# First pair's blocks inverted as halves of 16 tokens with a three-step solve, and a new order of the queues: a DeltaNet layer with a cosine-gated feed-forward

## The chip, the cores and the metric

The kernel runs on one core of one Trainium2 chip. The core has TensorE (PE, matmuls), VectorE (DVE), ScalarE (ACT), GpSimd (POOL) and SyncE (SP, which here only issues DMAs). The metric is the device time in microseconds of one launch.

## The reference

First a DeltaNet attention: 4 batches, 8 heads, 768 tokens, head size 48. Each head keeps a 48x48 state that is corrected token by token. Then each token's 384 features go through a feed-forward with 2048 hidden features and the gate h * cos(h).

```python
k_n = k / (norm(k) + 1e-06)
for t in range(S):
    y[:, :, t] = einsum('bhd,bhde->bhe', q[:, :, t], state)
    v_old      = einsum('bhde,bhd->bhe', state, k_n[:, :, t])
    state      = state + beta[:, :, t] * einsum('bhd,bhe->bhde', k_n[:, :, t], v[:, :, t] - v_old)
x = y as (3072 tokens, 384)
h = x @ w_in                 # 384 x 2048
out = (h * cos(h)) @ w_out   # 2048 x 384
```

The feed-forward weights arrive as float64 and are narrowed on the chip.

## The kernel before

**Tiling.** The 768 tokens of every head are cut into 24 units of 32 tokens (C = 32, unit n). Within a unit the token recursion is a unit triangular system: the Gram matrix of the unit's keys, scaled by beta, gives one 32x32 block for each of the 32 batch-head combinations. Two units make a pair m (12 pairs), whose 64 blocks are inverted together: half of the partitions holds the even rows of a block's inverse and the other half the odd ones.

**The recursion of one unit.** `turn` transposes keys and queries on TensorE (`turn_out` copies them on ScalarE). `gram` multiplies keys with keys and queries (L596). `gram_keys` scales the result on VectorE to `g` (L607), and `gram_put` sends `g` to memory (L634). For a pair, `gram_get` brings the blocks back as `gb`, with one block per partition (L643). `invert` runs over the 31 columns of the blocks with two instructions each, a product `part` and a subtraction from `z` (L672, L679). Pair 0 does this on VectorE with `z` in PSUM (`VECTOR = {0: "h"}`), the other pairs on GpSimd. `put` sends the inverse to memory (L688) and `get` brings it back as `zt` (L697). `solve` multiplies `zt` with the right-hand side (L745), `solve_out` scales it to `u` (L755), `update` and `update_out` change the state (L768, L776), `within` adds the unit's own part to its output (L785), and `features` transposes the output for the feed-forward (L804). `through_state` (L714) and `right_side` (L729) of the next unit need the new state.

**The feed-forward.** The pairs 0 and 1 run their hidden layer plainly: `hidden` (L825) makes 512 hidden features of 128 tokens with 12 matmuls, eight such groups to a pair, named by f = 0, 2, ..., 14. Pair 0 also has plain output groups (`output`, L970, four matmuls of 384 columns each). The later work uses a Strassen-like scheme (`layer`, L944, and `product`, L1027). Gating goes `turns` (ScalarE, L865), `rest` (VectorE, L872), `cos` (ScalarE, L881), `gate` (VectorE, L884).

**Weights.** There are 28 loads, 12 of w_in (512 KB) and 16 of w_out (384 KB). A load is `narrow_load` on SP (L465), `narrow_split` on ScalarE (L473, L475), `narrow_shift` on VectorE (L479, L484) and `narrow_add` on GpSimd (L488). A hidden group needs the adds of the w_in tiles up to its own part (f = 0 needs tiles 0 to 2, f = 6 needs all twelve); an output group needs those of w_out.

**What sets the order.** All tasks are handed to a list scheduler (`Order`) in the kernel's own source, each with an engine, a cost, a due time, the tasks it depends on, and the buffers it makes and frees. `Order.run` plays the engines with these costs and a model of DMA, and emits each task when its model starts it. The instructions of each engine, SP's included, then stay in exactly this order on the chip. `NUDGE` shifts due times by kind of task; the numbers were found by a search outside the kernel. The tag "g" is a pool of eight 4 KB buffers shared by weights, squares and gates.

Of the kernel before, what the change touches and what calls it, by code (L numbers as in the profile page):

```python
# [17 lines left out]
C = 32  # L18
# [7 lines left out]
def _consts():  # L26

    p = np.arange(128)
    share = p // 64
    row = SPLIT * np.arange(C // SPLIT)[None, :] + share[:, None]
    return np.concatenate(
        [
            np.eye(128),
            p[:, None] % C < np.arange(C)[None, :],
            p[:, None] // C % 2 == np.arange(2)[None, :],  # L40
            (row[:, :, None] == np.arange(C)).reshape(128, -1),
        ],
        axis=1,
    ).astype(np.float32)


class Order:
# [9 lines left out]
    WINDOW = 818.445  # L57
    LAG = {"PE": 0.2, "DVE": 0.15, "ACT": 0.15, "POOL": 0.2, "SP": 2.0, "IN": 0.0}
    IN_FLIGHT, ISSUE = 8, 0.49

    STEADY, LATE = 130.0, {"SP": 3.0, "POOL": 2.0}
    SLOW, WARM = 1.7, 4.0
    STICK = 1.823
    CHANGE = 0.15

    EARLY, NUDGE = 6, {('state', True): -3.4, ('features', False): -48.4, ('left', True): 37.6, ('solve', True): -19.7, ('turn', False): 12.2, ('within', True): -6.1, ('features_out', True): 39.0, ('rest', False): -12.6, ('weigh', False): -49.2, ('gram_put', True): 12.6, ('collect', False): -26.2, ('within', False): -32.5, ('features', True): -14.4, ('gate', True): -24.7, ('layer_out', False): -12.4, ('update', True): -10.5, ('sum', False): 24.3, ('layer', False): -1.8, ('add', True): -24.4, ('cos', True): 15.7, ('update', False): -6.1, ('solve', False): -34.1, ('norms', True): -9.2, ('state', False): -9.6, ('sum', True): 20.5, ('right', True): 24.7, ('hidden', True): 17.1, ('blocks', False): 2.6, ('gram', False): -8.1, ('inv_out', False): -15.0, ('v', False): 17.4, ('out', True): -13.0, ('eye', True): -0.5, ('features_out', False): -17.0, ('within_out', False): -0.6, ('gram_get', False): 12.2, ('gram_get', True): -21.0, ('turns', True): 8.1, ('scale', True): 5.8, ('k', True): -20.2, ('shift', True): -4.8, ('shift', False): 2.4, ('collect', True): 0.5, ('out', False): 0.3, ('scale', False): -1.8, ('out_out', True): 0.9, ('weigh', True): 5.0, ('store', True): -5.1, ('split', False): 9.0, ('within_out', True): -1.7, ('turns', False): -10.9, ('store_right', True): 3.6, ('turn_out', True): 1.5, ('k', False): 0.9, ('store_right', False): -5.1, ('inv', False): 5.4, ('square', False): 7.4, ('square', True): 4.1, ('norms', False): -1.3, ('store', False): 3.3, ('hidden', False): -4.1, ('cos', False): 3.4, ('x_sum', False): -0.6, ('beta_home', False): -1.9, ('store_left', True): -3.3, ('get', False): -6.1, ('get', True): 4.0, ('in_sums', False): 2.9, ('gram_queries', True): 1.6, ('turn_out', False): 5.0, ('update_out', False): -0.3, ('store_left', False): 0.1, ('inv', True): 1.1, ('v', True): -0.9, ('eye', False): -2.2, ('x_sum', True): 0.7, ('split', True): -3.1, ('beta_home', True): -4.7, ('weights', True): -0.3, ('gate', False): -3.7, ('put', False): -1.3, ('inv_out', True): -1.1, ('gram_keys', True): 0.6, ('solve_out', False): -1.5, ('add', False): 1.0, ('in_sums', True): 0.3}
# [5 lines left out]
    SMALL = ("gram", "state", "solve", "update", "within")  # L72
# [4 lines left out]
        "turn": 16, "gram": 128, "state": 256, "solve": 128, "update": 64, "within": 128,  # L77
# [8 lines left out]
    def add(  # L86
        self, key, engine, cost, emit, deps=(), makes=(), uses=(), moves=0.0, due=1e9
    ):

        assert key not in self.tasks, key  # L90
        self.tasks[key] = [engine, cost, due, emit, set(deps), makes, uses, moves]
        for t in uses:
            self.users[t] = self.users.get(t, 0) + 1
        for tag, t in makes:
            self.tiles[t] = tag
# [7 lines left out]

    def stall(self, key, now, commit):
# [5 lines left out]
        for i in range(self.written + 1, self.written + n + 1):  # L110
            t = now + cost * (i - self.written) / n + stall
            if (i + self.PHASE + self.AHEAD) % self.BLOCK == 0:
                there[(i + self.PHASE + self.AHEAD) // self.BLOCK + 1] = t + self.FETCH
# [10 lines left out]
    def run(self, wrote):  # L124
# [16 lines left out]
        for key, task in self.tasks.items():  # L141
# [3 lines left out]
            task[2] += self.NUDGE.get((key[0], n < self.EARLY), 0.0)  # L145
# [6 lines left out]
        flights, dma_free, hot = [5.5] * 4 + [8.5] * 4, 8.0, 1e9  # L152
        running, small = {}, False
        events = [(t, 0, None, False) for t in sorted(set(free.values()) | {0.0})]
# [3 lines left out]
        while events:  # L158
# [28 lines left out]
            for engine, heap in ready.items():  # L187
                if free[engine] > now:
                    continue
                able = [x for x in heap if x[0] <= limit and fits(x[2])]  # L190
# [39 lines left out]
                if moves:  # L230
                    end, parts = now, max(1, round(cost / self.ISSUE))
                    for _ in range(parts):
                        end = max(end, flights[-self.IN_FLIGHT]) + self.ISSUE
                        dma_free = max(dma_free, end + 0.5) + moves / parts
                        flights.append(dma_free + 1.4)
                    done = flights[-1]
# [12 lines left out]
def kernel(  # L249
# [85 lines left out]


# [14 lines left out]
    def qp(n):  # L351
        return qps[n // 2 % len(qps)][:, n % 2]

# [39 lines left out]
    near = 130 + C  # L393
# [4 lines left out]
    eye = consts[:, 130 + C :].rearrange("p (r i) -> p r i", i=C)  # L398
# [5 lines left out]
    nc.gpsimd.dma_start(out=consts[:, near:], in_=consts_dr.ap()[:, near:])  # L404

# [55 lines left out]
    def narrow_load(t):  # L461
# [3 lines left out]
        nc.sync.dma_start(out=words[t], in_=src)  # L465
# [147 lines left out]

    def gram_queries(n):
# [8 lines left out]
    def gram_put(n):  # L623
        m = n // 2
        if m not in gbs:
            gbs[m] = dram.tile([2, H, B, C, C], FP, name="g_dr")
# [6 lines left out]
        for rows, heads, bs in parts:  # L633
            nc.sync.dma_start(  # L634
# [3 lines left out]
    def gram_get(m):  # L638

        g_dr = gbs[m]  # L640
        gbs[m] = work.tile([128, C, C], FP, name="gb", bufs=GBS)
        for a in range(SPLIT):
            nc.sync.dma_start(  # L643
# [4 lines left out]
    def invert_eye(m, tag):  # L648
        if tag is None:
            zs[m] = work.tile([128, ROWS, C], FP, name="z", bufs=ZS)  # L650
        else:
            zs[m] = bank(tag, [128, ROWS, C], "p_i")
        nc.scalar.copy(zs[m], eye)

    def invert(m, tag, columns):
# [6 lines left out]
        for j in columns:  # L662
            rows = j // SPLIT + 1
            shape = [128, rows, C - 1 - j]
# [16 lines left out]
    def invert_out(m):  # L681
        z = work.tile([128, ROWS, C], FP, name="z", bufs=ZS)
        nc.scalar.copy(z, zs[m])
        zs[m] = z

    def put(m):
        z_drs[m] = dram.tile([ROWS, SPLIT, 2, H, B, C], FP, name="z_dr")
        nc.sync.dma_start(  # L688
# [3 lines left out]
    def get(n):  # L692

        zts[n] = work.tile([128, H, C], FP, name="zt")
        z_dr = z_drs[n // 2].rearrange("r s u h b i -> u b (r s) h i")[n % 2]
        for b in range(B):
            nc.sync.dma_start(out=zts[n][quarter(b)], in_=z_dr[b])  # L697
# [25 lines left out]
    def right_side(n):  # L723
# [10 lines left out]
        )  # L734

# [368 lines left out]
    W_IN, W_OUT, LOADS = 24.824, 4.888, 290.255  # L1104
    ONES, PLAIN = range(2), range(1)
    outs_done, collected, layered = [None], [None], [None]
    START = 41.528
    FIRST, STEP = 2.12, 3.854
    BASE = [START + (8 * FIRST + (p - 1) * 8 * STEP if p else 0) for p in range(NU // 2 + 2)]

    def inverse(m):
        add(("gram_get", m), "SP", 1.2, lambda: gram_get(m),
            [("gram_put", 2 * m), ("gram_put", 2 * m + 1)], makes=[("gb", ("gb", m))],
            uses=[("g_dr", m)], moves=1.6)
# [4 lines left out]
            makes=[(held or "z", z)])  # L1119
        deps = [("eye", m), ("gram_get", m)]  # L1120
        ends = [0, 4, 8, 12, 16, 20, 24, C - 1]
        for i, (x, y) in enumerate(zip(ends, ends[1:])):
            each = (0.2, 0.001) if held else (0.323, 0.00178)
            cost = sum(
                2 * (each[0] + each[1] * (j // SPLIT + 1) * (C - 1 - j)) for j in range(x, y)
# [3 lines left out]
                uses=[("gb", m)] if y == C - 1 else [])  # L1129
# [8 lines left out]
    def unit(n):  # L1138
        m, second = n // 2, n % 2
        for x, prev in (("k", 2 * len(kps)), ("q", 2 * len(qps)), ("v", 4)):  # L1140
# [7 lines left out]
            if x != "v" and n >= prev:  # L1148
# [5 lines left out]
                (x, n), "SP", 3.9 if x == "k" and n >= PLAIN_TURNS else 1.95,  # L1154
                lambda x=x: load(n, x), deps,
# [5 lines left out]
        if n < 4 or not second:  # L1161
# [8 lines left out]
            add(("scale", m, a), "DVE", 1.2, lambda: scale(m, part),  # L1170
                [("norms", m, a), ("beta",) if n < PLAIN_TURNS else ("beta_home",)])
        scaled = ("scale", m, a if n < 4 else 0)
        if second:
            add(("weigh", m), "DVE", 1.0 if n < PLAIN_TURNS else 1.35, lambda: weigh(m),
# [3 lines left out]
        if n < PLAIN_TURNS:  # L1178
            add(("turn", n), "PE", 0.9, lambda: turn(n, tag),
# [6 lines left out]
        else:  # L1186
            for a in range(2):
                deps = [("blocks", n - 1, a)] if n > PLAIN_TURNS else [("turn_out", n - 1)]
                deps.append(("turn_out", n - len(blocks)))
                add(("blocks", n, a), "SP", 1.9, lambda a=a: load_blocks(n, a), deps,  # L1190
# [4 lines left out]
        add(("gram", n), "PE", 0.75, lambda: gram(n, tag),  # L1195
# [5 lines left out]
            uses=[("p_g", n), ("scales", m)])  # L1201
        add(("gram_queries", n), "DVE", 0.46, lambda: gram_queries(n), [("gram_keys", n)],
            uses=[("p_g", n)])
        add(("gram_put", n), "SP", 0.45 if n < PLAIN_TURNS else 1.35, lambda: gram_put(n), [("gram_keys", n)],
            makes=[] if second else [("g_dr", ("g_dr", m))], uses=[("g_gram", n)],
            moves=0.85)
        if second:
            inverse(m)
        add(("get", n), "SP", 1.9, lambda: get(n), [("put", m)], makes=[("zt", ("zt", n))],
            uses=[("z_dr", m)], moves=0.9)  # L1210

        add(("state", n), "PE", 1.3 if n else 0.0, lambda: through_state(n),
# [5 lines left out]
        few = 0.75 if n < PLAIN_TURNS else 0.52  # L1218
        add(("solve", n), "PE", few, lambda: solve(n), [("right", n), ("get", n)],
            makes=[("two", ("p_u", n))], uses=[("zt", n), ("rhs", n) if n else ("vp", m)])  # L1220
# [12 lines left out]
        add(("features", n), "PE", 0.35, lambda: features(n), [("within_out", n)],  # L1233
# [5 lines left out]
    def gating(p, f, deps, uses, makes, due):  # L1239
        key = (p, f)  # L1240
        add(("turns", *key), "ACT", 0.65, lambda: hidden_turns(p, f), deps,
            makes=[("turns", ("turns", *key))])
        add(("rest", *key), "DVE", 0.73, lambda: hidden_rest(p, f), [("turns", *key)])
        add(("cos", *key), "ACT", 1.45, lambda: hidden_cos(p, f), [("rest", *key)])
# [17 lines left out]
    def gated(p):  # L1262
# [3 lines left out]
        for s in range(2):  # L1266
# [3 lines left out]
            for i in range(8):  # L1270
# [8 lines left out]
                add(key, "PE", 0.875 * count, lambda s=s, i=i: layer(p, s, i), deps,  # L1279
# [119 lines left out]
    def weights(t):  # L1399
        c = 1.0 if t < 12 else 0.8  # L1400
# [86 lines left out]
```

## Time and profile before

| what | value |
|---|---|
| time, median of 3 runs | 673.01 us (670.65 to 675.20) |
| the profiled execution | 673.73 us, its span 672.0 us |
| granted TensorE clock, mean | 0.992 |
| TensorE busy | 611.2 us (91%) |
| VectorE, ScalarE, GpSimd busy | 476.5, 246.6, 347.1 us |
| DMA | 52.55 MB, 215515 packets |

The page divides the span into 40 slices of 16.8 us and gives for each the busy share in tenths. A timeline row has start and length in us, the engine, the line, the operation, the output and inputs with their shapes, the count, and in brackets the idle time of the engine before it with what ended that. TensorE's float32 matmuls count twice in the trace, as each makes two passes. "PE", "DVE", "ACT" and "POOL" are the engines named above, and SPq is SP's queue of DMA issues.

### The profile page before, as it was taken

The page shows a single profiled execution, that of the slowest core. Times are in us where ns is not written, and L with a number is a line of the kernel's source. Part 1 is how long each engine was busy: PE and PEld are TensorE (multiplying, and loading weights), DVE is VectorE, ACT ScalarE, POOL GpSimd, SP SyncE. Part 2 cuts the span into 40 slices and gives each one's busy share as a digit, 9 for nine tenths or more (in the row PEclk, how much of TensorE's full clock was granted, in tenths as well). Part 3 has the DMA queues.
Part 4 walks back from the last instruction along what each step waited for, and adds up shares of the span by engine and source line. Part 5 has one row for each costly group of instructions (what it writes and reads, how often), then busy time and mean ns, then how long its engine had stood idle before and what let it go on. Part 6 is the DMA issues. An engine that isn't in the chain of part 4 may idle for free.

```text
span 672.0 us, 27226 instructions
## 1 busy us (share of the span) xinstructions
PE 611.2 (91%) x11864; PEld 572.8 (85%) x11864; DVE 476.5 (71%) x913; ACT 246.6 (37%) x414; POOL 347.1 (52%) x734
## 2 busy tenths in 40 slices
PE   4303798999999999999999999999999999999997
PEld 3202687986899999999999999999999999999996
DVE  5799498977676785886876876776766666656661
ACT  4432356551133342542432433433333334333420
POOL 4369797986848428587285383482382670000000
PEclk9999798999999999999999999999999999999999
DMA  8897655465453463434524524515213202000000
GB/s 179 198 199 158 155 130 161 103 115 90 68 96 65 63 101 59 90 56 68 109 36 60 113 34 65 107 26 92 56 21 57 56 7 54 1 4 24 1 24 24
DMA packets 215515, 52.55 MB, mean 78 GB/s; under 512 B 206948, under 2 KB 210164, under 8 KB 215396
## 3 DMA queue, kind: packets, MB, share of 16 engines
q1 hardware_dynamic: 212964, 49.98, 38.6%
q8 instruction: 93, 1.52, 1.0%
q10 hardware_dynamic: 2176, 0.39, 0.4%
q0 software_dynamic: 256, 0.44, 0.3%
q14 instruction: 26, 0.21, 0.1%
HBM read 39.76 MB, written 11.01 MB: 76 GB/s over the span
## 4 chain that ended last, share of the span: by engine, by line
PE 82%; POOL 7%; DMA 4%; DVE 2%; issue 2%; ACT 1%; SPq 1%; POOLq 0%; ACTq 0%
PE p_h L944 30%; PE p_out L1027 29%; PE p_kq L714 4%; PE p_h L825 4%; PE p_out L970 3%; PE p_u L745 2%; PE p_s L768 2%; PE p_kq L785 2%; PE p_g L596 2%; POOL part L672 2%; POOL z L679 2%; DMA gb<-g_dr 2%; POOL knrm L517 2%; PE p_o L1027 2%; POOL w_in L488 1%
## 5 line engine op out<-in xcount | busy, mean ns | idle before, releaser
L672 POOL TENSOR_TENSOR part<-z,gb 128x126 f32<-128x126 f32 (+22 forms) x341 | 136.0, 399 | 106.4 <-DMA gb<-g_dr 64.2
L679 POOL TENSOR_TENSOR z<-z,part 128x126 f32<-128x126 f32 (+22 forms) x341 | 137.3, 403 | 26.7
L944 PE MATMUL p_h<-x_ffn,w_in 128*128 128x128 f32 x1120 | 143.4, 277 | 0.0
L944 PEld LDWEIGHTS p_h<-x_ffn,w_in 128*128 128x128 f32 x1120 | 135.4, 192 | 1.2
L1027 PE MATMUL p_out<-w_out,g_ffn 128*128 128x192 f32 x672 | 123.8, 329 | 1.0 <-issue 1.0
L865 ACT ACTIVATE turns<-p_h,quarter_turn 128x512 int32<-128x512 f32 x96 | 65.8, 686 | 130.4 <-DVE p_h L963 96.2
L1027 PEld LDWEIGHTS p_out<-w_out,g_ffn 128*128 128x128 f32 x672 | 107.6, 190 | 1.7 <-issue 0.5
L1027 PE MATMUL p_out<-w_sum,g_ffn 128*128 128x192 f32 x496 | 91.6, 329 | 0.0
L881 ACT ACTIVATE turns<-turns,halfpi 128x512 f32<-128x512 f32 x96 | 69.1, 721 | 46.6 <-DVE turns L872 45.9
L872 DVE SCALAR_TENSOR_TENSOR turns<-p_h,turns 128x512 f32<-128x512 f32 x96 | 65.6, 684 | 23.4 <-ACT turns L865 23.3
L1027 PEld LDWEIGHTS p_out<-w_sum,g_ffn 128*128 128x128 f32 x496 | 79.3, 190 | 0.9
L1043 DVE TENSOR_TENSOR g_ffn<-g_ffn 128x512 f32<-128x512 f32 x88 | 63.2, 719 | 13.6 <-PE p_out L1027 13.3
L517 POOL TENSOR_TENSOR knrm<-ksum,halves 128x16 f32<-128x16 f32 (+1 forms) x14 | 37.2, 2657 | 66.7 <-DVE ksum L505 66.7
L884 DVE TENSOR_TENSOR g_ffn<-turns,p_h 128x512 f32<-128x512 f32 x96 | 65.0, 679 | 7.5 <-ACT turns L881 6.6
L963 DVE TENSOR_TENSOR p_h<-g_ffn,p_h 128x512 f32<-128x512 f32 x60 | 41.7, 695 | 40.0 <-PE p_h L944 37.9
L960 ACT COPY g_ffn<-p_h 128x512 f32<-128x512 f32 x60 | 35.1, 584 | 77.7 <-PE p_h L944 77.6
L825 PE MATMUL p_h<-x_ffn,w_in 128*128 128x128 f32 x384 | 47.6, 282 | 0.7 <-POOL w_in L488 0.6
L825 PEld LDWEIGHTS p_h<-x_ffn,w_in 128*128 128x128 f32 x384 | 45.2, 196 | 2.1 <-POOL w_in L488 1.1
L1077 DVE SCALAR_TENSOR_TENSOR o<-p_out,o 128x192 f32<-128x192 f32 x74 | 25.2, 353 | 28.9 <-PE p_out L1027 27.6
L944 PE MATMUL p_h<-x_sum,in_sum 128*128 128x128 f32 x320 | 43.7, 280 | 0.0
L944 PEld LDWEIGHTS p_h<-x_sum,in_sum 128*128 128x128 f32 x320 | 39.5, 192 | 1.1
L755 DVE TENSOR_TENSOR u<-p_u,bz 128x384 f32<-128x384 f32 x48 | 24.5, 552 | 14.9 <-PE p_u L745 14.6
(95 smaller groups left out, 759.0 us busy)
## 6 DMA issues: line engine op xcount, KB each, us to landing
pairs<-in_moe_w_in_dram SPq DMA_DIRECT2D x12, 512.0 KB
gb<-g_dr SPq DMA_DIRECT2D x24, 256.0 KB
pairs<-in_moe_w_out_dram SPq DMA_DIRECT2D x16, 384.0 KB
vp<-in_v_dram SPq DMA_DIRECT2D x96, 48.0 KB
out_dram<-o SPq DMA_DIRECT2D x23, 192.0 KB
z_dr<-z SPq DMA_DIRECT2D x12, 256.0 KB
zt<-z_dr SPq DMA_DIRECT2D x96, 32.0 KB
kp<-in_k_dram SPq DMA_DIRECT2D x128, 24.0 KB
```

What stands on the lines that cost most here:

```text
L517: nc.gpsimd.tensor_tensor(out=scales[m][2][:, part], in0=sums[m, part.start][:, 0:n], in1=halves[:, 0:n], op=ALU.pow,)
L672: eng.tensor_tensor(out=part, in0=z[:, 0:rows, j, None].to_broadcast(shape), in1=a[:, j, None, j + 1 :].to_broadcast(shape), op=ALU.mult,)
L679: eng.tensor_tensor(out=behind, in0=behind, in1=part, op=ALU.subtract)
L825: nc.tensor.matmul(p_h[:, i], w_in[:, t, (4 * k + i) * 128 : (4 * k + i + 1) * 128], xts[p][:, t, unit * 128 : (unit + 1) * 128], start=(t ...
L865: nc.scalar.activation(turns[p, f], hidden_of(p, f), AF.Identity, bias=quarter_turn, scale=TURN)
L872: nc.vector.scalar_tensor_tensor(out=r, in0=hidden_of(p, f), scalar=TURN, in1=t, op0=ALU.mult, op1=ALU.subtract,)
L881: nc.scalar.activation(r, r, AF.Sin, bias=halfpi, scale=2.0 * math.pi)
L884: nc.vector.tensor_tensor(out=place(p, f), in0=step_of(rests.pop((p, f)), f), in1=step_of(hidden_of(p, f), f), op=ALU.mult,)
L944: nc.tensor.matmul(p_h[:, e], in_sum[:, odd_tile, 4 * s + e] if a == "s" else w_in[:, a, f * 128 : (f + 1) * 128], x_sums[p][:, unit] if b ...
L963: nc.vector.tensor_tensor(out=block(p, s, 0, 1) if i == 3 else p_h, in0=block(p, s, *one), in1=p_h, op=ALU.add,)
L1027: nc.tensor.matmul(p_o, left(p, part, a)[:, e % 4], right(e, b), start=(e == 0), stop=(e == FT // 2 - 1), skip_group_check=True,)
L1043: nc.vector.tensor_tensor(out=left(p, s, to), in0=left(p, s, one), in1=left(p, s, two), op=op)
```

## The change

**Half blocks.** For pair 0 (`HALVED = 1`) a block of 32 tokens is no longer inverted whole. Its two diagonal 16x16 blocks are inverted instead; the block off the diagonal stays as it is and is used in the solve. `fold` puts the two diagonal blocks of a unit beside each other with three VectorE instructions, and writes the off-diagonal block to the tile `halves_z`, so `g` goes to memory at half the width. `gram_get` brings 16x16 blocks. `invert` runs over 15 columns. `put` and `get` move 16-wide rows, `get` with eight DMAs a unit in place of four.

**Three-step solve.** For units 0 and 1, `solve_half` multiplies the half inverses with the right-hand side, `half_out` copies the result on ScalarE, `between` multiplies it with the off-diagonal block, `between_out` subtracts that from the right-hand side on VectorE, and `solve` multiplies by the half inverses again. Each of the two new matmul steps has 32 matmuls (64 in the trace).

**Tiles.** `eye16` and the tile `halves_z` (off-diagonal blocks and half inverses of both units) take buffers of the tag "g" and are set on VectorE at the kernel's beginning.

**Order.** A table `ON_ACT` moves DMAs of the head from SP's queue to ScalarE's: two key loads, one query load, eight of the weight loads, one `gram_put`, three `gram_get` and pair 0's `put`; half of unit 0's `get` goes there too. The model of DMA in `Order.run` is a new one (rings, eight transfers in flight over both queues), costs, `NUDGE` and due times are new, and `HOLD` gives some fifty tasks a moment of the model before which they aren't taken. So the order of all engines differs from before. In the new order GpSimd adds w_in tiles 0 to 7 ahead of pair 1's inversion (before: 0 to 2 ahead of it), two w_in and two w_out adds within it, and two w_out adds and the last two w_in adds right behind it. TensorE gets four more groups of small matmuls; the fourth block (`gram_keys` of unit 3) comes behind the inversion of pair 0 on VectorE.

```diff
-    near = 130 + C
+    near = 132 + C
+    in_half = consts[:, 130 + C : 132 + C]
...
+    def fold(n):
+        g = gs.pop(n)
+        f = gs[n] = work.tile([128, H, HC], FP, name="fold", bufs=2)
+        nc.vector.tensor_scalar(f, g[:, :, 0:HC], in_half[:, 0:1], None, op0=ALU.mult)
+        nc.vector.scalar_tensor_tensor(
+            out=f, in0=g[:, :, HC:], scalar=in_half[:, 1:2], in1=f,
+            op0=ALU.mult, op1=ALU.add,
+        )
+        nc.vector.tensor_scalar(
+            off_blocks[n][:, :, HC:], g[:, :, HC:], in_half[:, 0:1], None, op0=ALU.mult
+        )
...
-            rows = j // SPLIT + 1
-            shape = [128, rows, C - 1 - j]
+            rows, last = j // SPLIT + 1, C
+            if m < HALVED:
+                rows, last = j + 1, HC
+            shape = [128, rows, last - 1 - j]
...
+        if n < 2 * HALVED:
+            zts[n] = half_zt[n]
+            for a in range(2):
+                for b in range(B):
+                    at = slice(C * b + HC * a, C * b + HC * a + HC)
+                    (nc.scalar if a and n == 0 else queue("get", n)).dma_start(
+                        out=zts[n][at, :, HC * a : HC * a + HC],
+                        in_=z_drs[n // 2][:, a, n % 2, :, b].rearrange("r h i -> r h i"),
+                    )
+            return
...
+    def solve_half(n):
+        triangular(n, "p_w", zts[n], rhss[n])
+    def half_out(n):
+        spare[n] = ffn_pool.tile([128, 2, H, D], FP, name="u_half", tag="g", bufs=GATES)
+        rest = first[n] = spare[n][:, 0]
+        nc.scalar.copy(by_parity(rest), p_us.pop(n))
+    def between(n):
+        triangular(n, "p_v", off_blocks[n], first.pop(n))
+    def between_out(n):
+        vt = rhss[n]
+        rhs = rhss[n] = spare.pop(n)[:, 1]
+        nc.vector.tensor_tensor(
+            out=by_parity(rhs), in0=by_parity(vt), in1=p_us.pop(n), op=ALU.subtract
+        )
...
+    ON_ACT = {('weights', 9): 1, ('gram_put', 0): 1, ('weights', 14): 1, ('weights', 3): 1, ('gram_get', 1): 1, ('k', 7): 1, ('k', 4): 1, ('q', 3): 1, ('weights', 10): 1, ('gram_get', 2): 1, ('weights', 15): 1, ('weights', 5): 1, ('weights', 17): 1, ('weights', 6): 1, ('put', 0): 1, ('gram_get', 0): 1}
```

## The prediction

> **What bounds the kernel now.** I read the busy slices of the page first, then busy time by stretch, then TensorE's timeline, then the timelines of the engines that feed it.
>
> ```profile
> PE   4303798999999999999999999999999999999997
> DMA  8897655465453463434524524515213202000000
> ```
> ```profile
> 113.69:667.10 553.41, 552.24 (x10376) 521.44 (x10375) 389.87 (x709) 198.88 (x328) 269.26 (x620) 1.00 0.33 60
> ```
> From 113.69 us to TensorE's last matmul at 667.10 us, TensorE (first figure after the length) is busy 552.24 of 553.41 us. There is nothing to win there but work. What can be won lies in the head, where the slices show 4303.
>
> ```profile
> 60.49 1.94 PE L745 MATMUL p_u<-vp,zt 32*32 32x48 f32 x64 [25.38 <-DMA zt<-z_dr]
> ...
> 76.02 4.01 PE L825 MATMUL p_h<-x_ffn,w_in 128*128 128x128 f32 x24
> ...
> 91.89 2.50 PE L825 MATMUL p_h<-x_ffn,w_in 128*128 128x128 f32 x20 [0.64 <-POOL w_in L488]
> ...
> 112.78 1.11 PE L565 MATMUL p_t<-consts,qp 128*128 128x128 f32 x4 [0.93 <-issue]
> 113.69 3.81 PE L970 MATMUL p_out<-w_out,g_ffn 128*128 128x384 f32 x8
> ```
> TensorE stands 25.38 us for the first inverse (zt), starts the feed-forward at 76.02, waits for a weight at 91.89, and reaches the second output group at 113.69. The waits before that group let the clock drop: 3.81 us against 2.75 us for the same group at 94.56.
>
> ```profile
> 27.71 0.19 DVE L672 TENSOR_TENSOR part_v<-p_i,gb 128x31 f32<-128x31 f32 x1 [1.22 <-DMA gb<-g_dr]
> ...
> 45.62 0.18 DVE L679 TENSOR_TENSOR p_i<-p_i,part_v 128x16 f32<-128x16 f32 x1
> ```
> ```profile
> 48.22 0.39 SPq L688 DMA_DIRECT2D z_dr<-z  x1
> 48.70 5.04 SPq L369 DMA_DIRECT2D qp<-in_q_dram  x4
> 53.79 1.93 SPq L369 DMA_DIRECT2D vp<-in_v_dram  x4
> 55.82 0.39 SPq L465 DMA_DIRECT2D pairs<-in_moe_w_in_dram  x1
> 56.26 4.24 SPq L697 DMA_DIRECT2D zt<-z_dr  x8
> ```
> The 25.38 us are thus 18.1 us of VectorE inversion (27.71 to 45.80) and 14.7 us of queue: the inverse is put at 48.22, but SP issues other loads until 56.26.
>
> ```profile
> 38.15 0.24 POOL L672 TENSOR_TENSOR part<-z,gb 128x31 f32<-128x31 f32 x1 [11.29 <-DMA gb<-g_dr]
> ...
> 78.54 0.23 POOL L679 TENSOR_TENSOR z<-z,part 128x16 f32<-128x16 f32 x1
> ...
> 111.99 1.98 POOL L488 TENSOR_TENSOR w_out<-w_out,pairs 128x384 uint32<-128x384 uint32 x2
> ```
> The second chain: GpSimd inverts pair 1 from 38.15 to 78.8 and also finishes every weight, up to the two w_out adds at 111.99, for which the group at 113.69 waits.
>
> **What the Trainium skill says.** "VectorE: DVE Perf Modes", section on the TRN2 errata: an instruction pays a fixed cost besides its elements. The trace agrees: 0.19 us at 30 elements, 0.29 at 126; so halving blocks saves mostly by halving the number of columns. "DMA: Bandwidth & Descriptors", section "Issuing engines are not separate DMA queues": issuing from a second engine saves only issue time. Here the DMA engines' busy share is 0.78 to 1.03 in each 10 us stretch up to 60, so moving loads to ScalarE frees SP but brings weights hardly earlier. "SBUF — State Buffer", section "Who interferes with whom": a VectorE instruction with two SBUF inputs blocks a GpSimd one that reads SBUF. The trace fits: three weight adds at 49.38 take 5.10 us, 1.70 each, against 1.28 alone. "TensorE: Matmul & The Clock Gate", Part 1: the clock halves after an idle window. Here the first hidden group takes 4.01 us, later ones 2.94.
>
> **The change part by part.**
> Tiles at the beginning: some 1300 elements of memset. From 768 elements in 0.70 us I work out 1.2 us; VectorE is idle 3.38 to 8.30. Free.
>
> Fold: three VectorE instructions of 128 to 256 elements per unit, not in the trace; between 0.17 (128x8) and 0.42 us (128x256) each. I take 0.25, so 0.75 for a unit and 1.5 in all. The second lies before the put: 1.2 us later at most. But the puts waited in SP until 17.98 although the second block was ready at 16.81, so nothing is lost; I leave the put at 17.7.
>
> Get of the blocks: 128 KB instead of 512. Before: first issue 22.79, first use 27.71. On ScalarE it waits for the weight split at 21.1 to 22.3 and for the put. I take issue at 22.5 and use at 25.2.
>
> Inversion: 15 columns of 15 to 64 elements. Column periods in the trace: 0.41 at 16, 0.45 at 30, 0.49 at 45, 0.52 at 58, 0.53 at 64 (between 58 and 78). Sum 7.3 us against 18.1. A weight's shift (1.1) and a scale (1.0) stand between: done at 34.6.
>
> Queue: copy and put go to ScalarE behind the split of the sixth weight; I take 36. The fourth block's put on SP waits for VectorE to finish the inversion (36.8), the half blocks' 16 gets (8 before) go half to SP, half to ScalarE, behind the get of pair 1. At 0.48 us an issue and 2 us to land, as at 58.3 to 60.4, the last useful get lands at 46 to 50. I take the first half-solve at 48, 12.5 us earlier.
>
> Three-step solve: per unit two more groups of 64 small matmuls, 0.88 us warm and 1.94 cold, with a ScalarE copy (0.46) and a VectorE subtraction (0.54) between. Unit 0: 1.94 + 0.46 + 1.94 + 0.54 + about 0.6 of hand-overs = 5.5 us more chain. Unit 1's extra 1.76 us lie among hidden groups. From solve to first hidden it was 15.5 us (60.49 to 76.02), so hidden starts at 48 + 5.5 + 15.5 = 69, 7 earlier.
>
> GpSimd is the part that takes it back. Pair 1's inversion now stands behind eight weight adds instead of three, so it starts after the eighth weight: loaded about 42, split 45.5, shifted 46.7, added 48. That is 10 us later than 38.15. Its 62 instructions cost 40.6 - 6.4 (four adds) - 3.4 (norm) = 30.8 us. With four adds between (2 x 1.3 + 2 x 1.0) and about 4.5 us of waits, since the split of one w_in tile stands on ScalarE behind unit 0's features and one w_out split behind the first cosine, it ends near 88 (48 + 30.8 + 4.6 + 4.5). Here the order matters: w_out tiles 14 and 15 (2.0) and the last two w_in adds (2.6) come after it: 92. So hidden group 4 (f = 6) starts near 92, against 90.55 before. TensorE has by then done the first output group, which it had not before, and four small groups more.
>
> From there to the second output group TensorE has 18.2 us: five hidden groups (14.5, the fourth to the eighth), a turn (0.7), solve, update and within (2.6), features (0.4). That is 110.2. GpSimd must by then have added w_out up to tile 19: 92.5 + norms 6.1 + 1.0 + wait for gb to about 100 + eight columns 7.0 + three adds 3.0 = 110. Both agree; I take 110.6 for the group that was at 113.69: 3.1 us gained.
>
> Work after this point: one hidden group less (2.94), one state group more (1.38), six switches between small and large groups fewer (146 against 152, about 0.1 each by 1.50 against 1.30 us for an output group after small and large), and 1.06 us of cold clock that shouldn't recur: 553.4 - 2.9 + 1.4 - 0.6 - 1.1 = 550.2. Tail after the last matmul 4.9 as before.
>
> Sum: 110.6 + 550.2 + 4.9 = 665.7 span; the profiled execution had 1.73 us around its span of 672.0 (673.73): 667.4. It stands 0.7 above the median of 673.01, which I leave, as single executions lie between 670.65 and 675.2.
>
> **Rivals.**
> A (forecast): 667.4, own range 664 to 671.
> B, GpSimd takes all back: if pair 1 starts at 52 rather than 48, or port blocking stretches the adds to 1.7, group 4 and the second output group slip by 4: 671.5. For it: GpSimd has 7.5 to 9.7 us busy of each 10 between 40 and 100. Against: it drops five adds to its idle 27 to 38.
> C, more than forecast: half-solve at 46, no ScalarE waits, the second output group at 106: 663. For it: the gap of SP behind the put was wholly order. Against: weights still arrive at DMA speed.
> D, slower: ScalarE becomes the bound. It now issues some 30 DMAs of the head in order, each of which can stand for an earlier transfer, with the splits, half_out and turns queued behind. SP shows the price: 5.04 us for four loads at 48.70, 3 beyond issue. Three such stands delay the half-solve and the eighth weight by 9, both chains together, so 676. It decides from 6.3 us of delay on, where the gain is gone. Against: ScalarE is busy only 3 to 5 of each 10 us there.
> E, the long stretch: a new order of all queues that starves TensorE after 113. It was without gaps, so it can only lose; 3 us would give 670.5. I have put it within A's and B's ranges.
>
> **How the numbers follow.** A 0.55, B 0.22, C 0.13, D 0.10. About 1% is what a measurement of this kernel tells from no change, that is below 666.3 or above 679.7. Faster by over 1%: all of C, nearly half of A, little of B: 0.40. Slower by over 1%: half of D and a bad stretch in E: 0.08. Within: 0.52. The range reaches from C's 661 to D's 676.
>
> **What would show it.** Right: first half-solve at 46 to 50, first hidden 67 to 71, GpSimd's pair 1 from 46 to 50 until 86 to 90, fourth hidden group at 90 to 94, second output group at 109 to 112, then no gaps. Wrong: ScalarE standing for DMA in front of half_out; a hidden or output group waiting on GpSimd's adds beyond 94 and 112; gaps of TensorE after 115.

## The result and the profile after

| | before | after |
|---|---|---|
| median of 20 runs each | 673.05 us (668.64 to 677.28) | 670.35 us (666.55 to 672.83) |
| the profiled execution, its span | 673.73, 672.0 us | 669.99, 668.2 us |
| second output group starts | 113.69 us | 109.07 us |
| from there to TensorE's last matmul: busy, idle | 552.24, 1.17 us | 549.64, 4.71 us |

The ratio is 0.9965 [0.995, 0.9979]: the change gains 2.7 us, where 5.6 us below the median shown before were forecast. A second set of runs of the kernel after gave 0.997 [0.9956, 0.9985].

TensorE's slices on the page after (busy share in tenths, 16.7 us to a slice):

```profile
PE   3316999999999999999999999999999999999997
```

In the first seven slices, the head, 3316999 stands where 4303798 stood: the third slice is no longer empty, and the slices are full from the fifth on instead of the eighth. TensorE's timeline shows the steps of the head:

```profile
49.32 1.81 PE L852 MATMUL p_w<-vp,halves_z 32*32 32x48 f32 x64 [1.16 <-ACT kq_t L634]
...
69.20 4.26 PE L965 MATMUL p_h<-x_ffn,w_in 128*128 128x128 f32 x24
...
91.47 2.72 PE L965 MATMUL p_h<-x_ffn,w_in 128*128 128x128 f32 x22 [1.06 <-POOL w_in L547]
...
109.07 2.10 PE L1110 MATMUL p_out<-w_out,g_ffn 128*128 128x384 f32 x6
111.51 0.91 PE L1110 MATMUL p_out<-w_out,g_ffn 128*128 128x384 f32 x2 [0.34 <-POOL w_out L547]
```

And GpSimd's timeline, the first and last step of pair 1's inversion and the last w_out add before the second output group ends:

```profile
49.75 0.23 POOL L765 TENSOR_TENSOR part<-z,gb 128x31 f32<-128x31 f32 x1
...
85.42 0.24 POOL L772 TENSOR_TENSOR z<-z,part 128x16 f32<-128x16 f32 x1
...
110.45 1.01 POOL L547 TENSOR_TENSOR w_out<-w_out,pairs 128x384 uint32<-128x384 uint32 x1
```

So the second output group starts 4.62 us earlier. The long stretch behind it became 0.94 us longer. Its row (length, TensorE busy, weight loads, then the other engines, clock, DMA share, GB/s):

```profile
109.07:663.30 554.23, 549.52 (x10481) 518.79 (x10479) 392.01 (x708) 197.37 (x327) 274.80 (x623) 1.00 0.33 61
```

The row stops 0.12 us short of the last matmul's end at 663.42, so TensorE's work there is 549.64 us. That is 2.60 us less than before, but it stood 4.71 us instead of 1.17. The waits of TensorE in this stretch, after (engine, group, what it waited for: us in all, times, longest):

```profile
PE p_h L1084 <- issue: 2.4, 3, 1.0
PE p_kq L822 <- issue: 0.8, 2, 0.5
PE p_out L1110 <- ACT o L1122: 0.6, 1, 0.6
PE p_out L1110 <- POOL w_out L547: 0.3, 1, 0.3
PE p_kq L925 <- issue: 0.3, 1, 0.3
PE p_out L1167 <- issue: 0.3, 1, 0.3
```

and the same view of the kernel before, from 113.69 us on, both in full:

```profile
PE p_out L1027 <- issue: 1.0, 2, 0.6
PE p_g L596 <- issue: 0.2, 1, 0.2
```

"issue" names no engine: all that the matmul needed was there. Such gaps are 3.80 us of the 4.71; the other two waits are 0.58 and 0.34. The tail behind the last matmul is 4.90 us before and 4.78 after. Together: -4.62 (head) - 2.60 (work) + 3.54 (idle) - 0.12 (tail) + 0.06 (around the span) = -3.74 us, the difference of the two profiled executions; the medians differ by less, as the profiled execution of the kernel before lay 0.7 above its median and that of the kernel after 0.4 below.

### The profile page after: what moved, and what is told of

Its sections match the earlier page's. It is cut to its first block, busy times and chain, and to the rows that moved or that the text cites. A ratio compares the mean times of both kernels' runs of the same rounds, so it can differ in the third digit from the quotient of the medians.

```text
span 668.2 us, 27726 instructions
## 1 busy us (share of the span) xinstructions
PE 615.3 (92%) x12120; PEld 576.3 (86%) x12120; DVE 470.1 (70%) x892; ACT 246.2 (37%) x416; POOL 348.5 (52%) x734
## 4 chain that ended last, share of the span: by engine, by line
PE 82%; POOL 5%; DMA 5%; DVE 4%; issue 2%; ACT 1%; SPq 1%; ACTq 0%; DVEq 0%; POOLq 0%
PE p_h L1084 31%; PE p_out L1167 29%; PE p_kq L822 4%; PE p_h L965 3%; PE p_out L1110 3%; PE p_s L908 2%; PE p_u L885 2%; PE p_kq L925 2%; PE p_g L655 2%; POOL part L765 2%; POOL z L772 2%; PE p_o L1167 2%; PE p_z L944 1%; DMA g_dr<-g 1%; DMA qp<-in_q_dram 1%
## 5 line engine op out<-in xcount | busy, mean ns | idle before, releaser
L1084 PE MATMUL p_h<-x_ffn,w_in 128*128 128x128 f32 x1120 | 145.5, 277 | 1.0 <-issue 1.0
L965 PE MATMUL p_h<-x_ffn,w_in 128*128 128x128 f32 x384 | 47.7, 283 | 1.5 <-POOL w_in L547 1.3
L624 PE MATMUL p_t<-consts,kp 128*128 128x128 f32 x32 | 7.4, 373 | 31.8 <-DMA halves_z<-z_dr 19.4
```

What stands on the lines that cost most here:

```text
L965: nc.tensor.matmul(p_h[:, i], w_in[:, t, (4 * k + i) * 128 : (4 * k + i + 1) * 128], xts[p][:, t, unit * 128 : (unit + 1) * 128], start=(t ...
L1084: nc.tensor.matmul(p_h[:, e], in_sum[:, odd_tile, 4 * s + e] if a == "s" else w_in[:, a, f * 128 : (f + 1) * 128], x_sums[p][:, unit] if b ...
```

## The experiments

Two theories for the "issue" gaps. O: the new order of the groups starves TensorE by itself. F: TensorE's instructions arrive in blocks, and a block that is needed right after a burst of small matmuls comes too late, as the burst has used up the block before it quickly.

**The same order at another place in the program.** Idle matmuls, whose results nothing uses, are put ahead of the turn of unit 4, while TensorE waits for the first inverse. Everything behind them keeps its order and lies 64, 128 or 192 instructions later. (An fp32 matmul is two passes, each a weight load and a multiplication: four instructions.)

```diff
     def turn(n, tag):
+        if n == 4:
+            for _ in range(16):      # 32 and 48 in the other two
+                nc.tensor.matmul(p_out[0:32, 0, 0:48], ident[0:32, 0:32], ident[0:32, 0:48])
```

> The changed kernel with 16 dummy matmuls (some 64 TensorE instructions, results overwritten later) put into TensorE's idle stretch at about 27 us; the order is otherwise the same. Question: the seven gaps marked 'issue' after 113 us (3.8 us in all, at 185.88, 254.73, 356.00, 379.22, 428.47, 445.79 and 600.88), which ate the gain. Theory F (instruction supply: TensorE's instructions come in blocks, and a gap opens where a block boundary falls right behind a burst of small matmuls): all boundaries move by 64 instructions, so the gaps leave these seven places, appear at others, and their sum changes, anywhere from 0.5 to 6 us; the time moves with it, 667 to 673. Rival O (the order itself starves TensorE at these groups): the same gaps at the same groups within 0.2 us, sum 3.5 to 4.1, time within 0.2% of the changed kernel (669 to 671.5).

> As the run with 64, with 32 dummy matmuls (some 128 instructions, half a block of 256). F: gaps move by 128 instructions, none is left at the seven places, sum 0.5 to 6 us. O: the same seven gaps, sum 3.5 to 4.1 us, 669 to 671.5.

> As the run with 64, with 48 dummy matmuls (some 192 instructions). F: gaps move by 192 instructions; at least one of the three shifted kernels has less than 2.5 us of such gaps after 113 us and is faster than the changed kernel by 1 us or more. O: the same seven gaps, 669 to 671.5.

The kernel before, shifted by 128:

> The kernel before with the same 32 dummy matmuls, in front of the turn of its fifth unit, where TensorE idles. It has 1.17 us of gaps after 113.69 us, three in number (175.78, 219.47, 450.20). F: they move; if the order before sat well on the boundaries by luck or search, the sum rises to 2 to 5 us and the time by 1 to 4 us (674 to 677). O: the same three gaps, time within 0.2% of before.

| kernel | median us | ratio to before | "issue" gaps after 120 us |
|---|---|---|---|
| before | 673.05 | 1 | 1.17 |
| after | 670.35 | 0.9965 [0.995, 0.9979] | 3.80 |
| after, 64 more | 692.46 | 1.025 [1.021, 1.0291] | 13.18 |
| after, 128 more | 695.85 | 1.0319 [1.028, 1.0359] | 16.40 |
| after, 192 more | 673.76 | 0.9987 [0.997, 1.0005] | 4.78 |
| before, 128 more | 683.24 | 1.011 [1.0068, 1.0151] | 9.05 |

Each ratio is to runs of the kernel before that were taken beside it, with a median of 673.05 us for the kernel after and 674.42 us for the shifts; the gaps are those of one profiled execution each. By these ratios an unchanged order lost 19 and 24 us in the first two shifts and 1.5 in the third, whose interval overlaps that of the kernel after. Its gaps went to other groups: O falls. The expected sizes were far too small, and no shift was faster.

The places say more. I counted each gap's place in TensorE's compiled program (waits that are instructions of their own included). In all thirteen traces of this study 106 gaps over 0.25 us, from 50 us on, are put down to "issue"; 104 of them begin at instruction 256k + 194 to 198, k a whole number. A gap of the kernel after, at instruction 6597 = 256 x 25 + 197:

```profile
181.94 1.36 PE L822 MATMUL p_kq<-st,kq_t 48*32 48x48 f32 x127
183.23 1.60 PE L1084 MATMUL p_h<-x_ffn,w_in 128*128 128x128 f32 x12
185.88 0.60 PE L1084 MATMUL p_h<-x_ffn,w_in 128*128 128x128 f32 x4 [1.05 <-issue]
```

The group of 16 is cut after 12, where no operand changes. What comes before is a burst: the 128 small matmuls of `through_state` are 256 instructions in some 1.4 us.

The blocks themselves are in the traces. The page lists the DMA queues with packets, MB and share of the engines; one queue carries instructions. Before and after:

```profile
q8 instruction: 93, 1.52, 1.0%
```
```profile
q8 instruction: 95, 1.56, 1.0%
```

Each of these packets has 16,384 bytes, which is 256 of the 64-byte instructions of TensorE's program (24,398 of them after, so 95 blocks). In the thirteen traces, from 50 us on, instruction 256k + 198 never started sooner than 1.2 us after the packet of its block had landed (packets and blocks counted in order), while instruction 256k + 195 sometimes ran before the landing. The 104 gaps ended 1.20 to 1.61 us after it; the packet for the gap at 185.88 landed at 184.42. So TensorE stood for its next block of instructions.

How long a block takes is less sure. From the six traces that I had then I fitted a rule for the gaps after 125 us: if the 306 instructions ahead of such a place took less than about 3.75 us, TensorE stands for the rest. Its mean error of 0.04 us a block counts the many blocks without a gap. Summed over a kernel the rule gives 13.1, 14.4 and 3.1 us for the three shifts, against 13.2, 16.4 and 4.8 measured, but only 1.4 of the 3.80 us of the kernel after. The packets show why a fixed 3.75 us can't fit: from 120 us on, a packet began 0.6 to 6.8 us (median 1.5) after the instruction 306 places ahead of its block had started. What makes this vary was not settled. The rule also says that of all shifts by 0 to 252 the kernel before has the least gaps at 0, and the kernel after at 236 to 240, that is 16 to 20 instructions earlier than it lies.

In the shift by 128 the gaps are about half of the loss. Another piece of it is seen behind a gap; the same group of 16 took 2.05 us in the kernel after:

```profile
231.61 1.09 PE L825 MATMUL p_kq<-st,kq_t 48*32 48x48 f32 x97
234.76 0.57 PE L825 MATMUL p_kq<-st,kq_t 48*32 48x48 f32 x30 [2.05 <-issue]
235.26 3.26 PE L1087 MATMUL p_h<-x_ffn,w_in 128*128 128x128 f32 x16
```

and by stretch, TensorE alone (length, busy, granted clock, DMA share, GB/s):

```profile
225.00:234.00 9.00, 7.70 (x209) 1.00 0.33 63
234.70:239.00 4.30, 4.24 (x52) 0.64 0.02 5
```

The clock falls with the gap. For the work that the kernel after does from 120 to 660 us, the shifted kernel has 12.6 us more of gaps and takes 7.1 us longer without them; four stretches of 3.4 us at half the clock, with none in the kernel after there, are worth up to 6.8 us of that. The remaining 6.1 of 25.9 us (between the profiled executions) came before 120 us, where the first half-solve ended 3 us later.

**The best shift.** 59 idle matmuls of four columns, 236 instructions:

```diff
+        if n == 4:
+            for _ in range(59):
+                nc.tensor.matmul(p_out[0:32, 0, 0:4], ident[0:32, 0:32], ident[0:32, 0:4])
```

> The kernel after, with 59 small matmuls (236 instructions, 4 columns each) added where TensorE idles at about 27 us. In the six traces so far every gap of TensorE over 0.25 us after 120 us that no other engine explains lies at instruction 256k + 195 to 198 of its program. Fitted on them: a gap opens when the last 306 instructions before such a place took less than about 3.75 us, and lasts the difference. By this rule, applied to the groups of the kernel after, a shift of 64, 128, 192 gives 13.1, 14.4, 3.1 us of gaps after 120 us (measured, without the one gap put down to ScalarE: 13.2, 16.4, 4.8), no shift 1.4 (measured 3.8), and 236 gives 0.1, the least with its neighbours. Theory F (supply in blocks of 256): gaps after 120 us 0.6 to 2 us, time 667 to 669.5. Theory O (the new order itself starves TensorE): 4 us or more of gaps at the same groups as in the kernel after, 670 or more.

Measured: "issue" gaps 2.04 us after 120, time 670.41 us, ratio 0.9958 [0.9941, 0.9975]; its profiled execution spans 666.5 us. The gaps fell by 1.8 us, less than the rule said, the time did not reach the 669.5 that F forecast, and the ratio can't be told from the 0.9965 of the kernel after. Its second output group started at 109.85, 0.8 later than in the kernel after. So I spread the same 59 over three idle places, and ran the kernel after beside it:

```diff
     def turn(n, tag):
+        for _ in range({2: 18, 3: 18, 4: 23}.get(n, 0)):
+            nc.tensor.matmul(p_out[0:32, 0, 0:4], ident[0:32, 0:32], ident[0:32, 0:4])
```

> The 59 added matmuls of the best shift in three idle places of TensorE (18 before the turn of unit 2, 18 before that of unit 3, 23 before that of unit 4) instead of all at about 28 us; from unit 4's turn on TensorE's program lies as in the kernel with 236 instructions more. Theory F: gaps after 120 us about 2 us again (measured 2.78 with the one behind ScalarE, against 4.38 in the kernel after). If the later second output group of that kernel (109.85 against 109.07) came from where the matmuls stood, it is at 109.1 now and the time 669 to 670; if it is chance of one execution, anything from 109 to 110, and 669 to 671. Against the kernel after, run beside it: 1 to 2 us faster by theory F.

> The kernel after once more, unchanged, on the same chip as the shifted one, for a direct comparison and for the spread of its head: 669.5 to 671.5, gaps after 120 us 4 to 5 us at the same instructions (theory F), second output group at 108.5 to 110.5.

Measured: 668.63 us, 0.9954 [0.9937, 0.997], against 670.95 for the kernel after beside it (21 and 22 runs). The ratio of these two medians is 0.9965; drawing the runs again with replacement gives [0.9957, 0.9985]. "issue" gaps after 120 us: 2.15 and 3.89. The second output group started at 109.26 and 109.75, so the 0.8 above lies within what executions differ by. With 59 matmuls in one place or in three, the ratio to the kernel before is the lowest of the study (0.9958 and 0.9954): the kernel after with instructions that do nothing. Only the second was run beside the kernel after, and was 2.3 us faster; its trace has 1.7 us less of "issue" gaps.

The gaps of one program differ between executions. In the repeated kernel after, four of its seven gaps over 0.25 us came back at the same instructions, three did not, and one of 1.18 us at 135.14 is new; it too lies at a block's beginning. In the trace of the spread version the group shown above is whole:

```profile
183.16 2.05 PE L1086 MATMUL p_h<-x_ffn,w_in 128*128 128x128 f32 x16
```

**Is the supply slowed by other DMAs?** The kernel with 128 instructions more, without the transposed loads of keys and queries from unit 10 on:

```diff
+        if n >= PLAIN_TURNS + 2:
+            return
```

> The kernel with 128 instructions more (16.98 us of gaps after 120 us) with the transposed loads of keys and queries left out from unit 10 on, so that the DMA engines are nearly free after 120 us; TensorE's program is the same. If the supply of TensorE's blocks is slowed by that traffic, the gaps after 120 us fall below 10 us; if each block takes its 3.75 us anyway, they stay at 14 to 18 us.

Waits of TensorE after 120 us with the loads, then without them (the largest two of each):

```profile
PE p_kq L825 <- issue: 14.1, 10, 2.3
PE p_kq L928 <- issue: 1.4, 1, 1.4
```
```profile
PE p_kq L827 <- issue: 13.4, 10, 2.0
PE p_kq L930 <- issue: 2.0, 2, 1.1
```

All "issue" gaps after 120 us: 16.12 us against 16.40 with the loads, the DMA engines busy 0.25 against 0.33 of the time. So these loads are not what delays the blocks. This is one execution of each. The DMA traffic fell only by a quarter, not to nearly nothing as expected, so a dependence on the rest of it stays possible.

**The second queue.** All DMA issues back on SP, TensorE's order unchanged:

```diff
-        return nc.scalar if key in Order.ON_ACT else nc.sync
+        return nc.sync
...
-                    (nc.scalar if a and n == 0 else queue("get", n)).dma_start(
+                    queue("get", n).dma_start(
```

> The kernel after with every DMA issue of ScalarE put back on SP, in the same places of the order; TensorE's order is unchanged, and its program is one instruction longer. If the second queue carries the gain of the head: half-solve 2 to 6 us later than 49.32, GpSimd's pair 1 later than 49.75, total 672 to 676. If it does not matter (issue time only): within 1 us in both, total 669.5 to 671.5. Gaps after 120 us stay near 4 us by theory F, as the blocks lie the same.

675.0 us, 1.0023 [1.0009, 1.0038]: against the kernel after's 0.9965 this is 0.6% slower, about 3.9 us. But not as expected: the half-solve (49.01) and GpSimd's pair 1 (48.40) were not late. What was late is a load of keys, which SP issued at 66.41. ScalarE squares them ahead of unit 0's last copy, which it then does at 72.41:

```profile
70.57 0.84 ACT L559 ACTIVATE ksq<-kp 128x768 f32<-128x768 f32 x1 [8.64 <-DMA kp<-in_k_dram]
```
```profile
72.95 1.90 PE L852 MATMUL p_w<-rhs,halves_z 32*32 32x48 f32 x64 [7.01 <-ACT x_ffn L952]
74.78 1.44 PE L965 MATMUL p_h<-x_ffn,w_in 128*128 128x128 f32 x5
```

TensorE waits 7.01 us for that copy, and the first hidden group comes at 74.78 instead of 69.20. The early inverse was there, and the wait for SP's other loads took it back. The "issue" gaps after 120 us stayed at 4.05; those over 0.25 us are at five of the seven groups of the kernel after, as F says for blocks that lie the same.

**Pair 0 whole in the new kernel.** `HALVED = 0`, and the tile `eye16` with its task left out.

```diff
-    HALVED, HC = 1, C // 2
+    HALVED, HC = 0, C // 2
...
-    add(("eye16",), "IN", 0.1, lambda: None, [("q", 1)], makes=[("g", ("eye16",))])
```

> The kernel after with HALVED = 0: pair 0 is inverted whole as before, no fold and no three-step solve, all else of the new scheduler, tables and ScalarE queue kept; the scheduler writes a new order. Theory H (the halving itself shortens the head): inversion again 18 us on VectorE, first solve at 55 to 60, first hidden group at 71 to 75 against 69.20. Theory Q (the order and the second queue do it): first hidden group at 70 or earlier. Gaps after 120 us fall as the blocks of 256 happen to lie, 1 to 15 us, so the total says little; 668 to 685.

692.84 us, 1.0293 [1.0268, 1.0319], and no answer: the scheduler's tables fit the halved kernel, and the order that they gave without it is bad in itself. Two sets of query loads hold SP for 12 us, and the first solve waits for its gets, which come after them:

```profile
49.87 12.37 SPq L418 DMA_DIRECT2D qp<-in_q_dram  x8
```
```profile
68.61 0.33 PE L881 MATMUL p_u<-vp,zt 32*32 32x48 f32 x2 [7.26 <-DMA zt<-z_dr]
```

**An early inverse in the old kernel.** The kernel before, with pair 0's put and unit 0's gets issued on ScalarE right behind each other:

```diff
     def put(m):
-        nc.sync.dma_start(
+        (nc.sync if m else nc.scalar).dma_start(
...
+        if m == 0:
+            get(0, nc.scalar)
```

> The kernel before with six lines changed: pair 0's put and the four gets of unit 0 are issued on ScalarE, the gets right behind the put, instead of on SP with two sets of loads between them. Nothing is halved and no other order changes; TensorE's order is the same and its program is 3 instructions longer, so gaps after 120 us stay at 1 to 2 us. First solve at 53 to 56 (before: 60.49), first hidden group at 68 to 71 (76.02). Theory P (GpSimd's adds and its pair 1 inversion set the end of the head): the hidden group that waited for w_in at 91.89 starts within 1 us of that, the second output group at 112 to 114, time within 1.5 us of the kernel before. Theory S (the start of TensorE's chain sets it): everything moves by 5 us or more and the time is 667 to 669, as good as with the halving.

The first solve began at 52.55 and, after a wait for the rest of `zt`, ran from 54.83 instead of 60.49. Nothing came of it:

```profile
63.36 0.83 DVE L479 SCALAR_TENSOR_TENSOR pairs<-pairs 128x512 uint32<-128x512 uint32 x1 [1.02 <-ACT pairs L475]
...
64.69 1.01 DVE L759 TENSOR_TENSOR u<-p_u,bz 128x384 f32<-128x384 f32 x2
```
```profile
65.84 1.56 PE L772 MATMUL p_s<-u,kp 64*64 64x96 f32 x32 [8.99 <-DVE knrm L528]
```

The solve was done at 56.9, but VectorE took `solve_out` (writing `u`) only at 64.69: its order has the shift of a weight right ahead of it. In the kernel before, that shift ended at 62.48, just when the solve ended too; here it ends at 64.77, as the loads of SP and the splits of ScalarE came 2 us later (one split had stood 7.14 us behind the gets, 54.61 against 52.18). TensorE waited 8.99 us, the first hidden group started at 75.80 (76.02 before), the second output group at 113.31, and the time was 676.47 us, 1.0054 [1.0028, 1.008]. S fails, as the earlier start moved nothing. P's two places held (the hidden group at 91.14, the second output group), but not for P's reason: that hidden group no longer waited for a weight. What held the start was the fixed order of VectorE and ScalarE. Why the median is 4 us longer while the profiled execution is only 0.5 longer is not explained.

## Why the prediction was right or wrong

| step | forecast | measured |
|---|---|---|
| first half-solve | 48 (46 to 50) | 49.32 |
| first hidden group | 69 (67 to 71) | 69.20 |
| GpSimd's pair 1, start and end | 48, 88 | 49.75, 85.66 |
| fourth hidden group | 92 (90 to 94) | 89.92, with 1.06 of wait at 91.47 |
| second output group | 110.6 (109 to 112) | 109.07 |
| rest of TensorE's work, busy | 549.0 | 549.64 |
| rest, idle | 1.2 | 4.71 |
| tail | 4.9 | 4.8 |

The forecast's 550.2 for the rest starts from 553.4, which is a length and holds the 1.17 us of idle time before. So it is 549.0 of work and 1.2 of idle time, though the text speaks of no gaps.

**Right.** The head, step by step, within 2.4 us each, and TensorE's work behind it within 0.7. The end of pair 1 and the fourth hidden group came just ahead of their ranges. That the first hidden group came within 0.2 us is in part luck: the half-solve was 1.3 late, and the way from it to the hidden group took 19.88 us instead of 21.0. The 15.5 us in that sum were taken from the profile before with 4.47 us of "issue" gaps in them; after, such gaps were 2.31 there. One reading was wrong without harm: 18.1 and 14.7 us make 32.8, from 27.71 to 60.49, and not the 25.38 that TensorE stood, as it had work until 35.1. Smaller terms: the use of the half blocks began at 28.46 (forecast 25.2; VectorE waited 2.34 us for them), and the put went out at 37.81 (36); of the gets behind it, SP's were issued only from 45.21 on. The folds took 0.91 us a unit (0.75).

**Wrong.** The step "Work after this point", which let the idle time of the stretch stay as it was while the order changed, and with it rival E. The prediction named it ("a new order of all queues that starves TensorE after 113", "3 us would give 670.5") and then put it within the ranges of A and B instead of giving it a chance. 3.54 us more of idle time and 0.6 more of work, less 1.5 in the head and 0.1 in the tail, is the distance from 667.4 to 669.99 but for rounding. The reason given there, that the stretch "was without gaps, so it can only lose", pointed the right way: the direction was known, the size was set at nothing. The mechanism was not named at all. TensorE was not starved by the other engines' queues: 3.80 of the 4.71 us are blocks of instructions that came late, as the shifts and the instruction packets show. The new order counts in that it sets which groups lie where the blocks begin.

That such gaps exist could have been read beforehand. The profile before has gaps "issue" of 2.10 us at 70.71 and 0.93 at 112.78, which I took for nothing:

```profile
70.71 0.72 PE L714 MATMUL p_kq<-st,kq_t 48*32 48x48 f32 x55 [2.10 <-issue]
```

And the scheduler's own `stall` counts blocks of 256 instructions (`BLOCK, PHASE, AHEAD, FETCH = 256, 63, 38, 3.5`) and picks groups around them. Both orders were thus made for their blocks where they lie, which fits that no shift of 64 to 192 instructions gained. The change adds four groups of 128 instructions and a new order, so every later block falls elsewhere. The fitted rule (place 194 to 198, 306 instructions ahead, 3.75 us) is close to these constants (193, 256 + 38, 3.5). Why the scheduler's count let these gaps through in the kernel after stays open.

**The rivals.** D (ScalarE as the bound) did not occur: in the kernel after TensorE waited 1.32 us at 67.41 for a copy of ScalarE, which had stood 4.80 us for a query load. In the old order with gets on ScalarE a stand of 7.14 us was part of what cost the gain. B (GpSimd takes all back) did not occur: the waits for it in front of TensorE are 0.21, 1.06 and 0.34 us. The second output group, at 109.07, lies between A's 110.6 and C's 106, nearer to A's.

**Left open.** What the halving is worth without the new order: the kernel with it switched off has a bad order of its own. What is shown is that this order loses its gain without the second queue (3.9 us), and that an earlier inverse alone, in the old order, gains nothing. An order made for one queue was not tried. What sets the time of an instruction packet is open too.

## What to carry to other kernels

A gap that a trace puts down to no engine is a finding, not noise: count where it lies in the engine's instruction stream before explaining it by the order. Where TensorE runs small matmuls, adding or removing a few groups moves every later block of instructions, so a change in one place must be charged for gaps everywhere behind it; some idle instructions where the engine waits anyway test this cheaply, and the packets of the instruction queue confirm it. And an earlier result is worth only what the queues of all the engines behind it are ordered to take.

## What the runs showed of the hardware

TensorE's instructions came in packets of 16,384 bytes here, 256 to a packet, and a block's first instructions ran at the earliest 1.2 us after its packet had landed. 128 small matmul passes used a block up in 1.4 us. A gap cost 0.3 to 2.9 us, and the gaps of a kernel after 120 us up to 16.40 us.

Such a gap can cost twice. The Trainium skill ("TensorE: Matmul & The Clock Gate", Part 1) puts the fall to the half clock after an idle window of about 3.4 us. Here the clock fell with gaps shorter than that, though not each time, and whether the small matmuls ahead of them had a part in it was not separated: after 2.05 us at 234.76 (128 more) the clock was 0.62 over the next 4 us, after 2.13 us at 357.97 (the kernel before with 128 more) 0.50, but after 2.56 us at 193.47 (64 more) it stayed at 1.00.
